# A fused attention and gated-MLP kernel: two scalar loads moved late, 24 unread TensorE products ahead of the first score product

## The chip, the core and the metric

The kernel runs on one core of one Trainium2 chip. The metric is the device time of one execution in microseconds (us); lower is better. The kernel before takes 443.92 us (median of three runs, 441.65 to 444.85).

Engines are named as in the profile: PE is TensorE (PEld its weight loads), DVE is VectorE, ACT is ScalarE, POOL is GpSimd, SP is SyncE, whose queue (SPq) issues nearly all the loads and stores here.

## What is computed

```python
# B, H, S, D = 4, 8, 768, 64; d_model 512, d_ff 1024; n_sink = 4, window = 128 (both int64 inputs)
scores = q @ k.T / sqrt(D)
keep   = (key < n_sink) | (0 <= query - key < window)
a      = softmax(where(keep, scores, -1e9))
x      = (a @ v) laid out as (B, S, H * D)
h      = relu(x @ w_in);  u, v = h[..., :512], h[..., 512:]
v_n    = (v - mean(v)) / sqrt(var(v) + 1e-6)          # over the 512 features
out    = (u * (w_spatial @ v_n + b_spatial)) @ w_out
```

The two scalars n_sink and window are run-time inputs. The kernel has a fast path for the pair (4, 128) and a general path for every other pair; the general path runs after the fast one if a flag says that the pair is another one. In the profiled run the pair is (4, 128), so only the fast path does work.

## The kernel before

Attention is cut into 48 half tiles: 4 batches, 6 tiles of 128 queries, two halves of 4 heads. For each half tile PE makes the score products (`sc`, L881 for batch 0 and L887 for the others), DVE adds the mask and takes the row maxima (`pexp` and `nm`, L892), ACT takes the exponentials (L897), the result is transposed (`tr` on PE and `pT` copies for batch 0, DMA transposes for the others), PE makes the products with v (`av`), and DVE divides (`den`, `x`, L1020 to L1024). For every tile of 128 rows there follow the product with the v half of w_in (`ps_v`, then relu, variance and the normalised `vn`), for every 256 rows the product with the u half (`ps_u`), and once a batch has all its `vn`, the spatial product (`ps_s` from `wsp` and `vn`), the gate `g`, and the last product (`ps_o`).

The weights arrive as 64-bit words. `w_in` and `w_out` are decoded in pieces of 128x512 on ACT (L663, L665), DVE (L661 or L659, L669, L671) and POOL (L674); `w_in` and `wsp` are then split into a high and a low 16-bit half on ACT (L576) and DVE (L597).

The order of all this work is made by a planner. Each piece of work is added with a rank, the engine or engines that may do it, an estimated time and the tiles that it reads and writes (`plan.add`). `Plan.order()` then goes through the pieces greedily: it takes the piece that can begin first by its own estimates, gives it the engine that would end it first, and books the ring of buffers that its tiles live in. The result is one fixed order for each engine. Each engine then works through its own instructions in order and waits where data is not there yet. PSUM has 8 banks: 4 for `sc` and `tr`, 2 for one `av` buffer, and 2 for a ring called `mm` that holds `ps_v`, `ps_u`, `ps_s`, `ps_o` and the small products of the maxima (`ps_row`, `ps_col`).

Ahead of the plan stand `begin` (masks, an identity and other constants, most of it on POOL) and `read_scalars` (L35), which loads the two scalars to all 128 partitions as 128 pieces of 8 bytes each, one load on SP's queue (L38) and one on ACT's (L39), and converts them on DVE (L41). The comparison with (4, 128) is written behind the fast path (L1211 to L1215: four comparisons, a maximum, a conversion), and every engine reads the flag into a register (L1216). On DVE the conversion and the comparison stand in the order ahead of the first `pexp`; on SP the flag is read between two loads of `w_in`. The first loads of the plan are those of the first keys (`wsp<-qk_t`, L836; for batch 0 the keys lie in room that later holds `wsp`), the first queries (`qkraw<-qk_t`, L602), and four pieces of `w_in` (`dec<-w_in`).

Of the kernel before, what the change touches and what calls it, by code (L numbers as in the profile page):

```python
# [6 lines left out]
F32 = mybir.dt.float32  # L7
F32R = mybir.dt.float32r
F16 = mybir.dt.float16
BF16 = mybir.dt.bfloat16  # L10
I32 = mybir.dt.int32
U32 = mybir.dt.uint32
AF = mybir.ActivationFunctionType
ALU = mybir.AluOpType
AX = mybir.AxisListType
# [4 lines left out]
P = 128  # L20
# [11 lines left out]
EXP_HIGH = bits_as_f32(0x47F00000)  # L32


def read_scalars(tc, pool, n_sink, window):  # L35
    nc = tc.nc
    words = pool.tile([P, 4], I32, name="words")
    nc.sync.dma_start(words[:, 0:2], n_sink.bitcast(I32).partition_broadcast(P))  # L38
    nc.scalar.dma_start(words[:, 2:4], window.bitcast(I32).partition_broadcast(P))  # L39
    wf = pool.tile([P, 4], F32, name="wf")  # L40
    nc.vector.tensor_copy(wf, words)  # L41
    return words, wf


def f64_to_f32(nc, raw, w, tmp, top=None):
# [218 lines left out]
TOGETHER0 = 4  # L264
FIRST_LOADS = (('q', 0), ('w', 0), ('w', 1), ('w', 2), ('w', 3), ('v', 0), ('q', 1), ('v', 2), ('v', 4), ('v', 5))
IN_TURN = ("u", "vn", "qkraw", "qp", "pexp", "pT", "p16", "xT", "x16", "av", "sc", "vraw", "vslot0", "vslot1", "vslot2", "vslot3")
LATENCY = {"PE": 0.25, "d": 0.15, "a": 0.18, "p": 0.12}


# [7 lines left out]


QUEUED = 3.0
class Plan:  # L280


# [4 lines left out]
    def __init__(self, rings, ring_of):  # L287
        self.pieces, self.rings, self.ring_of = [], rings, ring_of
# [5 lines left out]
    def order(self):  # L294
# [40 lines left out]
        def room(i):  # L335

            t, new = 0.0, {}
            for key in ps[i][5] + ps[i][6]:
# [4 lines left out]
                k = len(held[ring]) + new.get(ring, 0)  # L343
                if ring in IN_TURN and turn[ring][k] != base:
                    return None
# [7 lines left out]
        while open_:  # L353
            best = None
            for i in open_:
# [4 lines left out]
                if ps[i][7] and not ps[i][5]:  # L360
                    t = max(t, moved - QUEUED)
                es = ps[i][2] if ps[i][2] not in free else (ps[i][2],)
# [20 lines left out]
            if dma is None:  # L383
                end = t + d + LATENCY[e]
            else:
# [30 lines left out]
def begin(nc, pool):  # L416


    st = Begin()
    first = pool.tile([P, 1], F32, name="first")  # L420
    nc.vector.memset(first, 0.0)
    nc.scalar.activation(first, first, AF.Exp)
    st.wsp = pool.tile([P, (NT + 1) * S], F32, name="wsp")
    st.wout = pool.tile([P, 2, KC, DM], F32R, name="wout")
    st.vflat = pool.tile([P, NV * 2 * H * (D + 1)], F16, name="vring")
    st.vring = vring = st.vflat.rearrange("p (s i h d) -> p s i h d", s=NV, i=2, h=H)

    def cur_mask(m):
        nc.gpsimd.affine_select(out=m, in_=m, pattern=[[-1, P]], compare_op=ALU.is_ge,
                                fill=NEG, base=0, channel_multiplier=1)  # L430

    def prev_mask(m):
        nc.gpsimd.affine_select(out=m, in_=m, pattern=[[1, P]], compare_op=ALU.is_gt,
                                fill=NEG, base=0, channel_multiplier=-1)

    m_first = pool.tile([P, P], BF16, name="m_first")
    nc.gpsimd.memset(m_first, 0.0)
    cur_mask(m_first)
    nc.gpsimd.memset(m_first[:, :NS], 0.0)
    m_odd = pool.tile([P, 2, SEG], BF16, name="m_odd")  # L440
    m_even = pool.tile([P, 2, SEG], BF16, name="m_even")
    m_second = pool.tile([P, 2, SEG], BF16, name="m_second")
    for m, cur in ((m_odd, 1), (m_even, 0), (m_second, 1)):
        nc.gpsimd.memset(m, 0.0)
        cur_mask(m[:, cur, 2:])
        prev_mask(m[:, 1 - cur, 2:])
    nc.gpsimd.memset(m_second[:, :, :2], NEG)
    nc.gpsimd.memset(m_second[:, 0, 2:2 + NS], 0.0)

    st.ident = pool.tile([P, P], F32, name="ident")  # L450
    make_identity(nc, st.ident)
    st.ones = pool.tile([1, P], F32, name="ones")
    nc.vector.memset(st.ones, 1.0)
    mhalf = pool.tile([P, 1], F32, name="mhalf")
    nc.vector.memset(mhalf, -0.5)
    b_bc = pool.tile([P, S], F32, name="b_bc")
    st.masks = m_first, m_second, m_even, m_odd
    st.mhalf, st.b_bc = mhalf, b_bc
    return st


def fast_path(tc, st, qk, v, v0, vs, w_in, w_sp, b_sp, w_out, out):

# [1 line left out]
    nc = tc.nc  # L467
    TC = 256
    VNS = 2.0 ** 10
    with (  # L470
# [42 lines left out]
        def bank(tag):  # L513
            return lambda name: ps_all.tile([P, 512], F32, tag=tag, name=name, bufs=BANKS[tag])
# [3 lines left out]
        def next_p16(name):  # L518
# [21 lines left out]
            "sc": ("sc", bank("sc")), "tr": ("sc", bank("sc")),  # L540
            "av": ("av", lambda name: ps_all.tile([P, 1024], F32, tag="av", name=name, bufs=BANKS["av"])),
            "ps_v": ("mm", bank("mm")), "ps_u": ("mm", bank("mm")), "ps_s": ("mm", bank("mm")),
            "ps_o": ("mm", bank("mm")), "ps_row": ("mm", bank("mm")), "ps_col": ("mm", bank("mm")),
        }
        rings = {"u": UB, "vn": VNB, "vr": VB, "vraw": VRB, "vsraw": 1, "qkraw": QKB, "qp": QPB, "pexp": PEB,
                 "p16": P16B, "pT": PTB, "x": 1, "x16": 2, "xT": XTB, "g": 2, "g2": G2B,
# [2 lines left out]
        plan = Plan(rings, dict({k: r for k, (r, _) in makers.items()}, **{r: r for r in rings}))  # L549
# [277 lines left out]
        def whole(b):  # L827
            return b < WHOLE
# [330 lines left out]
                     [("ob", i)], [], dma=0.8)  # L1159


        W = WHEN
        for t in (0, 2, 4, 5):
            load_v(t)
        w_in_half(1)
# [4 lines left out]
        for i, (b, t, hf) in enumerate(subs):  # L1170
            n = TOGETHER0 if whole(b) else TOGETHER
            for h2 in range(0, HH, n):
                scores(i, b, t, hf, h2, i - W["score"] + h2 * W["pair"], n)
            weights(i, b, t, hf, i - W["split"])
            attend(i, b, t, hf, i)
            if hf == 0:
                queries_keys(b, t, early.get(("q", t), i - W["load"]) if b == 0 else i - W["load"], i - W["qk"])
                if not whole(b):
                    value(b, t, i - W["value"])
                if t == 0:  # L1180
                    v_scale(b, i - W["vscale"])
                continue
            v_half(b, t, i + W["v"])
            if t % 2:
# [17 lines left out]
def tile_kernel(tc, qk, v, v0, vs, n_sink, window, w_in, w_sp, b_sp, w_out, out):  # L1202
    nc = tc.nc
    with tc.tile_pool(name="top", bufs=1) as top:
        with tc.tile_pool(name="first", bufs=1) as pool:
            st = begin(nc, pool)
            words, wf = read_scalars(tc, top, n_sink, window)
            fast_path(tc, st, qk, v, v0, vs, w_in, w_sp, b_sp, w_out, out)
        bad = top.tile([P, 4], F32, name="bad")
        for i, x in enumerate((FAST_N, 0, FAST_W, 0)):  # L1210
            nc.vector.tensor_scalar(bad[:, i:i + 1], wf[:, i:i + 1], float(x), None, op0=ALU.not_equal)  # L1211
        flag = top.tile([P, 1], F32, name="flag")
        nc.vector.tensor_reduce(out=flag, in_=bad, axis=AX.X, op=ALU.max)
        flagi = top.tile([P, 1], I32, name="flagi")
        nc.vector.tensor_copy(flagi, flag)  # L1215
        rv = nc.values_load(flagi[0:1, 0:1], min_val=0, max_val=1)  # L1216
        with tc.If(rv > 0):
            general_path(tc, wf, qk, v, w_in, w_sp, b_sp, w_out, out)

FAST_N, FAST_W = 4, 128  # L1220

# [42 lines left out]
```

## Time and profile before

| what | us |
|---|---|
| median of three runs | 443.92 (441.65 to 444.85) |
| span of the profiled execution, first to last instruction of the program | 439.1 |
| PE busy | 414.1 (94%) |
| DVE busy | 319.1 (73%) |
| ACT busy | 272.0 (62%) |
| POOL busy | 156.6 (36%) |

The rest of a run, about 4.8 us against the median, lies around the span. The engines run beside each other, so shares of busy time do not add up; what counts is who waits for whom. The chain that ended last is 85% PE and 9% DVE by time. PE is not busy for the first 7.4 us, is partly busy up to about 40 us, and is then busy nearly all the time, with short stops between 100 and 130 us, until 432 us.

### The profile page before, as it was taken

To read this page: it belongs to the slowest core of one execution; us is meant where nothing else is said; L and a number is where in the kernel's file an instruction comes from. 1 tells how busy PE (TensorE), PEld (TensorE's weight loads), DVE (VectorE), ACT (ScalarE), POOL (GpSimd) and SP (SyncE) were. 2 spreads that over 40 slices of the span, in tenths; PEclk is the share of its full clock that TensorE was granted. 3 is DMA by queue.
4 is the path that set the end of the run, shared out by engine and by line. 5 is a ranking of instruction groups with operands and counts; after the bars stand their busy time and mean duration, and the time that the engine had idled before them with its cause. 6 is when DMAs were issued, how large, how long until landed. Compare 5 with 4: busy or idle time off the path is not lost.

```text
span 439.1 us, 9802 instructions
## 1 busy us (share of the span) xinstructions
PE 414.1 (94%) x3669; PEld 323.9 (74%) x3669; DVE 319.1 (73%) x937; ACT 272.0 (62%) x584; POOL 156.6 (36%) x214
## 2 busy tenths in 40 slices
PE   2689999999989999999999999999999999999994
PEld 1467777777677877877778878868778778688882
DVE  3999988689999885878986966788994645143430
ACT  3898978789977565469864754677664353232211
POOL 4426565645735432238351512343541112000000
PEclk9999999999999999999999999999999999999998
DMA  5999414549976784279964673567723822200011
GB/s 215 384 344 296 119 29 115 169 118 196 175 132 162 182 173 133 41 209 208 189 170 123 134 154 87 73 187 154 135 69 98 137 61 64 73 2 24 25 48 57
DMA packets 117928, 59.98 MB, mean 137 GB/s; under 512 B 100240, under 2 KB 103920, under 8 KB 117872
## 3 DMA queue, kind: packets, MB, share of 16 engines
q1 hardware_dynamic: 117728, 59.27, 55.3%
q8 instruction: 31, 0.51, 0.5%
q14 instruction: 25, 0.20, 0.1%
q10 hardware_dynamic: 144, 0.00, 0.0%
HBM read 28.58 MB, written 6.29 MB: 79 GB/s over the span
## 4 chain that ended last, share of the span: by engine, by line
PE 85%; DVE 9%; DMA 2%; issue 1%; ACT 1%; POOL 0%; SPq 0%; ACTq 0%; DVEq 0%
PE ps_s L608 21%; PE ps_o L608 16%; PE ps_v L608 13%; PE ps_u L608 12%; PE sc L887 6%; PE av L1013 4%; PE sc L881 3%; DVE pexp L892 2%; PE tr L925 2%; PE av L997 1%; PE av L999 1%; PE av L998 1%; DMA qkraw<-qk_t 1%; PE av L1005 1%; DVE wsp L597 1%
## 5 line engine op out<-in xcount | busy, mean ns | idle before, releaser
L608 PE MATMUL ps_s<-wsp,vn 128*128 128x256 f16 x864 | 101.0, 273 | 1.6 <-DVE wsp L597 0.8
L608 PEld LDWEIGHTS <-vn 128*128 128x128 f16 x864 | 82.5, 98 | 14.8 <-issue 2.7
L897 ACT ACTIVATE pexp<-pexp,nm 128x260 f32<-128x260 f32 (+1 forms) x192 | 81.2, 484 | 6.2 <-DVE nm L892 6.0
L608 PE MATMUL ps_o<-wout,g 128*128 128x512 f32 x288 | 70.2, 399 | 0.0
L608 PE MATMUL ps_u<-xT,win 128*128 128x256 f16 x576 | 69.0, 273 | 0.4 <-ACT u L1110 0.4
L608 PE MATMUL ps_v<-win,xT 128*128 128x512 f16 x288 | 66.2, 379 | 1.1 <-ACT u L1110 1.1
L608 PEld LDWEIGHTS ps_o<-wout,g 128*128 128x128 f32 x288 | 53.1, 188 | 12.8
L608 PEld LDWEIGHTS <-win 128*128 128x128 f16 x576 | 54.9, 98 | 10.0 <-issue 1.7
L1131 DVE SCALAR_TENSOR_TENSOR g<-ps_s,isc,b_bc 128x256 f32<-128x256 f32 x48 | 23.1, 481 | 39.6 <-PE ps_s L608 38.2
L608 PEld LDWEIGHTS <-xT 128*128 128x128 f16 x288 | 27.0, 98 | 31.5 <-issue 2.2
L574 ACT CAST g<-g 128x256 fp32r<-128x256 f32 x39 | 15.8, 404 | 50.5 <-DVE g L1135 48.3
L590 DVE TENSOR_TENSOR p<-pexp,p 128x1024 f16<-128x1024 f32 (+2 forms) x56 | 40.6, 747 | 8.6 <-ACT p L574 8.6
L590 POOL TENSOR_TENSOR x<-x,x 128x512 f16<-128x512 f32 x24 | 31.2, 1299 | 22.5 <-ACT x L574 21.4
L887 PE MATMUL sc<-kring,qp 64*128 64x260 f32 (+1 forms) x432 | 35.3, 296 | 0.0
L1110 ACT ACTIVATE u<-ps_u,icu 128x256 f32<-128x256 f32 x48 | 22.3, 469 | 17.2 <-PE ps_u L608 17.2
L887 PEld LDWEIGHTS sc<-kring,qp 64*128 64x128 f32 x432 | 28.1, 186 | 6.3 <-issue 4.2
L1078 POOL TENSOR_TENSOR rs<-rs,mhalf 128x1 f32<-128x1 f32 x24 | 16.2, 676 | 46.0 <-DVE rs L1072 42.5
L1157 ACT COPY ob<-ps_o 128x512 f32<-128x512 f32 x24 | 14.1, 586 | 27.9 <-PE ps_o L608 27.9
L574 ACT CAST p<-pexp 128x32 f16<-128x32 f32 (+2 forms) x52 | 30.7, 620 | 0.5
L1068 DVE BATCH_NORM_STATS2 st<-vr 128x6 f32<-128x512 f32 x24 | 16.5, 689 | 17.2 <-ACT vr L1062 17.2
L590 DVE TENSOR_TENSOR g<-g,g 128x256 fp32r<-128x256 f32 x41 | 22.5, 550 | 8.5 <-ACT g L574 7.9
L997 PE MATMUL av<-vring,pT 128*128 128x65 f16 x264 | 27.7, 193 | 0.0
(143 smaller groups left out, 762.5 us busy)
## 6 DMA issues: line engine op xcount, KB each, us to landing
qkraw<-qk_t SPq DMA_DIRECT2D x18, 512.0 KB, 4.4
out<-ob SPq DMA_DIRECT2D x24, 256.0 KB, 2.3
vraw<-v_s SPq DMA_DIRECT2D x18, 256.0 KB, 4.4
dec<-w_in SPq DMA_DIRECT2D x8, 512.0 KB, 6.9
wsp<-w_sp_t SPq DMA_DIRECT2D x6, 384.0 KB, 6.1
dec<-w_out SPq DMA_DIRECT2D x4, 512.0 KB, 4.5
wsp<-qk_t SPq DMA_DIRECT2D x6, 256.0 KB, 5.5
qkraw<-qk_t SPq DMA_DIRECT2D x6, 256.0 KB, 4.4
```

Of the source, the lines that this page charges most:

```text
L574: nc.scalar.copy(o, x)
L590: eng[e].tensor_tensor(out=o, in0=x, in1=hi, op=ALU.subtract)
L608: nc.tensor.matmul(o, a, m, start=(i == 0), stop=(i == n - 1))
L887: nc.tensor.matmul(o, qp[rows, qi, hp, :], keys(kring[:, ki], rows), start=(m == 0), stop=(m == 2))
L897: nc.scalar.activation(po, po, AF.Exp, bias=nm()[:, h2 + q:h2 + q + 1], scale=-1.0)
L997: nc.tensor.matmul(o[:, h], ph, vh, start=(t < 2 and j == 0), stop=False)
L1013: nc.tensor.matmul(o[:, h], pT[:, q * P:(q + 1) * P], v_whole(kt)[:, g:g + D + 1], start=(t < 2 and j == 0), stop=(j == nb - 1 and (t < 2 ...
L1068: nc.vector.bn_stats(s6, vr())
L1078: nc.gpsimd.tensor_tensor(out=vals["rs", i], in0=vals["rs", i], in1=mhalf, op=ALU.pow)
L1110: plan.add(r + WHEN["u relu"], "a", 0.36, lambda e: nc.scalar.activation(tl("u", (b, c0))[:, d, :], tl("ps_u", i)[:, :TC], AF.Relu, scale= ...
L1131: nc.vector.scalar_tensor_tensor(out=g(), in0=tl("ps_s", i)[:, :TC], scalar=vals["s", "sp"][1], in1=b_bc[:, t0:t0 + TC], op0=ALU.mult, op1 ...
L1157: plan.add(r + WHEN["o copy"], "a", 0.5, lambda e: nc.scalar.copy(tl("ob", i), tl("ps_o", i)), [("ps_o", i)], [("ob", i)])
```

## The change

Two things. First, the loads of the scalars, their conversion and their comparison become two pieces of the plan at rank 27 (`SCALARS_AT`): both loads on SP, the comparison on DVE. The flag is still read where its user stands, on every engine. Second, `begin` writes a tile `warm` of 128x512 bf16 numbers with an `iota` on POOL, and the plan gets one piece at rank -300, ahead of all others: 24 products of 128x128 with 128x256 of that tile into one bank of the `mm` ring. Nothing reads that bank. The rank table `WHEN` is the same.

```diff
-def read_scalars(tc, pool, n_sink, window):
-    nc = tc.nc
-    words = pool.tile([P, 4], I32, name="words")
-    nc.sync.dma_start(words[:, 0:2], n_sink.bitcast(I32).partition_broadcast(P))
-    nc.scalar.dma_start(words[:, 2:4], window.bitcast(I32).partition_broadcast(P))
-    wf = pool.tile([P, 4], F32, name="wf")
-    nc.vector.tensor_copy(wf, words)
-    return words, wf
+class Scalars:
+    def __init__(self, nc, pool, n_sink, window):
...
+    def load(self):
+        for i, x in enumerate(self.sources):
+            self.nc.sync.dma_start(self.words[:, 2 * i:2 * i + 2], x.bitcast(I32).partition_broadcast(P))
+
+    def compare(self):
+        v = self.nc.vector
+        v.tensor_copy(self.wf, self.words)
+        for i, x in enumerate((FAST_N, 0, FAST_W, 0)):
+            v.tensor_scalar(self.bad[:, i:i + 1], self.wf[:, i:i + 1], float(x), None, op0=ALU.not_equal)
+        v.tensor_reduce(out=self.flag, in_=self.bad, axis=AX.X, op=ALU.max)
+        v.tensor_copy(self.flagi, self.flag)
...
+WARM_N, WARM_FIRST = 256, 24
+SCALARS_AT = 27.0
...
+    st.warm = pool.tile([P, 512], BF16, name="warm")
+    nc.gpsimd.iota(st.warm, pattern=[[1, 512]], base=1, channel_multiplier=3, allow_small_or_imprecise_dtypes=True)
...
+        def keep_warm(n):
+            for _ in range(n):
+                nc.tensor.matmul(tl("warm", 0)[:, :WARM_N], st.warm[:, :P], st.warm[:, :WARM_N], start=True, stop=True)
+
+        plan.add(-300, "PE", 0.1, lambda e: keep_warm(WARM_FIRST), [], [("warm", 0)])
+        plan.add(SCALARS_AT, "SP", 0.8, lambda e: scalars.load(), [], [("words", 0)], dma=0.3)
+        plan.add(SCALARS_AT, "d", 1.3, lambda e: scalars.compare(), [("words", 0)], [("flag", 0)])
...
-            words, wf = read_scalars(tc, top, n_sink, window)
...
-        bad = top.tile([P, 4], F32, name="bad")
-        for i, x in enumerate((FAST_N, 0, FAST_W, 0)):
-            nc.vector.tensor_scalar(bad[:, i:i + 1], wf[:, i:i + 1], float(x), None, op0=ALU.not_equal)
...
```

The start of SP's queue, before and then with the change (`wsp<-qk_t` is the load of the first keys, `qkraw<-qk_t` that of the first queries, `dec<-w_in` a piece of 64-bit weights, `vring<-v_ones` two tiles of v):

```order
L1260 UNCONDITIONAL_BRANCH
L38 DMA words<-n_sink 128x2
L836 DMA wsp<-qk_t 128x4x128
L602 DMA qkraw<-qk_t 128x512
L602 DMA dec<-w_in 128x1024 x4
L801 DMA vring<-v_ones 128x2x520
```

```order
L1278 UNCONDITIONAL_BRANCH
L854 DMA wsp<-qk_t 128x4x128
L620 DMA qkraw<-qk_t 128x512
L620 DMA dec<-w_in 128x1024 x4
L819 DMA vring<-v_ones 128x2x520
L854 DMA wsp<-qk_t 128x4x128
```

The load of the scalar ahead of the first keys is gone; the rest stands as it did.

The last of the 24 products on PE and what follows them, with the change (before, the `sc` row is PE's first):

```order
L1182 LDWEIGHTS warm
L1182 MATMUL warm<-warm 128x256
L1182 LDWEIGHTS warm
L1182 MATMUL warm<-warm 128x256
L899 MATMUL sc<-wsp,qkraw 128x128 x8
L943 MATMUL tr<-ident,pexp 128x128 x4
L1031 MATMUL av<-vring,pT 128x65 x4
```

All 24 stand ahead of the first score products. On POOL the `iota` stands ahead of the masks.

DVE where the comparison now stands, about 63 us into the span of before (`w` is a piece of w_out being decoded, `vr` and `vn` the normalised v half), before and then with the change:

```order
L1086 TENSOR_SCALAR vr<-vr,mv,rs 128x512
L671 SCALAR_TENSOR_TENSOR w_751<-dec,w_751 128x512
L590 TENSOR_TENSOR vn<-vr,vn 128x512
L892 ISA pexp,nm<-sc,m_even 128x260
L892 ISA nm 128x1
```

```order
L1104 TENSOR_SCALAR vr<-vr,mv,rs 128x512
L689 SCALAR_TENSOR_TENSOR w_780<-dec,w_780 128x512
L52 CAST wf<-words 128x4
L54 TENSOR_SCALAR bad<-wf 128x1 x4
L55 TENSOR_REDUCE flag<-bad 128x1
L56 CAST flagi<-flag 128x1
L910 ISA pexp,nm<-sc,m_even 128x260
L910 ISA nm 128x1
```

The seven instructions of the scalars have come in, and the subtraction for `vn` has gone from here to POOL. Up to this place every engine's order is the same but for the moved and the new instructions. From here to the order's place at about 155 us in before the planner orders the pieces differently: on PE one `ps_v` and several `ps_u` groups of twelve change places with half tiles of attention, with the same number of `ps_v` and `ps_u` groups ahead of the first `ps_s`; and some pieces change engines (over the whole order DVE has two fewer 128x512 copies or casts, ACT two fewer `p16` casts of 128x1024 and two fewer `kring` casts, POOL two more casts of each of the latter two kinds). Behind that the orders are the same again.

## Rows read from the trace of the kernel before

**Rows 1.** The page, busy time of each engine: busy us, share of the span, instructions.

```profile
PE 414.1 (94%) x3669; PEld 323.9 (74%) x3669; DVE 319.1 (73%) x937; ACT 272.0 (62%) x584; POOL 156.6 (36%) x214
```

**Rows 2.** Busy time by stretch. Columns: stretch, its length; then busy us (and instructions) of PE, PEld, DVE, ACT, POOL; granted TensorE clock, share of the DMA engines, GB/s.

```profile
5.00:10.00 5.00, 2.52 (x16) 2.10 (x16) 2.44 (x17) 1.40 (x3) 0.80 (x6) 1.00 1.02 389
10.00:20.00 10.00, 5.28 (x22) 3.89 (x23) 9.72 (x30) 8.88 (x20) 5.19 (x4) 1.00 1.05 383
20.00:30.00 10.00, 8.10 (x32) 5.48 (x29) 9.50 (x35) 10.00 (x23) 1.47 (x2) 1.00 0.96 348
30.00:40.00 10.00, 9.59 (x66) 7.84 (x65) 9.38 (x32) 7.54 (x17) 5.75 (x8) 1.00 1.04 302
40.00:60.00 20.00, 20.00 (x135) 14.12 (x134) 18.71 (x61) 18.51 (x39) 12.32 (x18) 1.00 0.49 139
```

**Rows 3.** The same columns, stretches of 1 us at the start.

```profile
4.00:5.00 1.00, 0.00 (x0) 0.00 (x0) 0.00 (x0) 0.00 (x0) 0.41 (x3) 1.00 0.17 7
5.00:6.00 1.00, 0.00 (x0) 0.00 (x0) 0.36 (x5) 0.00 (x0) 0.00 (x0) 1.00 0.96 293
```

**Rows 4.** The timeline of the start: start us, us, engine, line, operation, out<-in, count, and in brackets the idle time before it and what ended it.

```profile
0.72 0.20 POOL L437 MEMSET m_first<- 128x128 bf16 x1 [0.29 <-POOLq L1254]
0.72 0.40 SPq L38 DMA_DIRECT2D words<-n_sink  x1
1.90 0.60 SPq L602 DMA_DIRECT2D qkraw<-qk_t  x1
2.20 0.31 POOL L444 MEMSET m_second<- 128x260 bf16 x1
4.12 0.29 POOL masks.py:199 TENSOR_SCALAR_AFFINE_SELECT ident<-ident 128x128 f32<-128x128 f32 x1
5.60 0.17 DVE L41 CAST wf<-words 128x4 f32<-128x4 int32 x1 [4.59 <-DMA words<-n_sink]
6.36 0.15 DVE L1215 CAST flagi<-flag 128x1 int32<-128x1 f32 x1
7.43 2.70 PE L881 MATMUL sc<-wsp,qkraw 64*128 64x128 f32 x16 [7.43 <-DMA qkraw<-qk_t]
8.35 0.29 DVE L892 CUSTOM_DVE_ANT_0 pexp<-sc,m_first 128x128 f32<-128x128 f32 x1 [1.83 <-PE sc L881]
```

**Rows 5.** DMA issues of the stretch 0 to 2.5 us, and (last row) of 49 to 51 us: out<-in, queue, operation, count, KB, us from issue to landing.

```profile
qkraw<-qk_t SPq DMA_DIRECT2D x1, 256.0 KB, 5.4
words<-n_sink SPq DMA_DIRECT2D x1, 1.0 KB, 4.8
...
qkraw<-qk_t SPq DMA_DIRECT2D x1, 256.0 KB, 3.5
```

**Rows 6.** PE's timeline, the same form of product early and later (columns as in rows 4).

```profile
29.46 1.91 PE L925 MATMUL tr<-ident,pexp 128*128 128x128 f32 x8
...
39.83 1.04 PE L925 MATMUL tr<-ident,pexp 128*128 128x128 f32 x8
```

**Rows 7.** The chain that ended last, stretch 0 to 45 us, in order of time: start us, us, what; and its rows at 60.76 us and at 85.16 us, where the first score products of batch 1 begin.

```profile
21.06 3.98 DMA wsp<-qk_t
...
25.08 2.68 PE sc L881 x7
...
60.76 2.62 PE ps_u L608 x24
...
85.16 0.81 PE sc L887 x12
```

**Rows 8.** The page, POOL's costliest 128x512 operation: busy us, mean ns, idle before it.

```profile
L590 POOL TENSOR_TENSOR x<-x,x 128x512 f16<-128x512 f32 x24 | 31.2, 1299 | 22.5 <-ACT x L574 21.4
```

**Rows 9.** SP and DVE at 44 and around 64 us (timeline), and SP's read of the flag (one line's instructions: count, ns least/median/most, first and last start us).

```profile
43.68 1.26 SPq L1041 DMA_TRANSPOSE xT<-x  x1
...
64.52 0.39 SPq L602 DMA_DIRECT2D qkraw<-qk_t  x1
...
63.12 1.55 DVE L590 TENSOR_TENSOR vn<-vr,vn 128x512 f16<-128x512 f32 x1 [0.35 <-ACT vn L574]
64.59 0.41 DVE L892 CUSTOM_DVE_ANT_0 pexp<-sc,m_even 128x260 f32<-128x260 f32 x1
...
L1216 SPq TENSOR_LOAD <-flagi x1: 476/476/476, 15.2 to 15.2; - x1
```

**Rows 10.** What PE waited for from 42 to 160 us (us, times, longest), and two rows of POOL and the chain there.

```profile
PE ps_v L608 <- ACT u L1110: 1.1, 1, 1.1
PE ps_s L608 <- DVE wsp L597: 0.8, 1, 0.8
PE ps_s L608 <- ACT wsp L576: 0.5, 1, 0.5
PE ps_u L608 <- ACT u L1110: 0.4, 1, 0.4
PE ps_s L608 <- DVE g L1131: 0.3, 1, 0.3
PE ps_col L635 <- DVE allmax L632: 0.3, 1, 0.3
...
128.18 2.12 PE ps_s L608 x18
...
110.70 2.06 POOL L590 TENSOR_TENSOR p<-pexp,p 128x1024 f16<-128x1024 f32 x1
```

More of the change, by code (lines that the diff above doesn't have):

```diff
@@ L32 @@
 EXP_HIGH = bits_as_f32(0x47F00000)
-def read_scalars(tc, pool, n_sink, window):
-    nc = tc.nc
-    words = pool.tile([P, 4], I32, name="words")
-    nc.sync.dma_start(words[:, 0:2], n_sink.bitcast(I32).partition_broadcast(P))
-    nc.scalar.dma_start(words[:, 2:4], window.bitcast(I32).partition_broadcast(P))
-    wf = pool.tile([P, 4], F32, name="wf")
-    nc.vector.tensor_copy(wf, words)
-    return words, wf
+class Scalars:
+    def __init__(self, nc, pool, n_sink, window):
+        self.nc, self.sources = nc, (n_sink, window)
+        self.words = pool.tile([P, 4], I32, name="words")
+        self.wf = pool.tile([P, 4], F32, name="wf")
+        self.bad = pool.tile([P, 4], F32, name="bad")
+        self.flag = pool.tile([P, 1], F32, name="flag")
+        self.flagi = pool.tile([P, 1], I32, name="flagi")
+    def load(self):
[8 more added lines that the diff above has]
+        v.tensor_copy(self.flagi, self.flag)
 def f64_to_f32(nc, raw, w, tmp, top=None):
@@ L459, in begin, with fast_path @@
     return st
-def fast_path(tc, st, qk, v, v0, vs, w_in, w_sp, b_sp, w_out, out):
+def fast_path(tc, st, scalars, qk, v, v0, vs, w_in, w_sp, b_sp, w_out, out):
     nc = tc.nc
@@ L542, in fast_path @@
             "ps_v": ("mm", bank("mm")), "ps_u": ("mm", bank("mm")), "ps_s": ("mm", bank("mm")),
-            "ps_o": ("mm", bank("mm")), "ps_row": ("mm", bank("mm")), "ps_col": ("mm", bank("mm")),
+            "ps_o": ("mm", bank("mm")), "warm": ("mm", bank("mm")), "ps_row": ("mm", bank("mm")), "ps_col": ("mm", bank("mm")),
         }
@@ L1206, in tile_kernel @@
             st = begin(nc, pool)
-            words, wf = read_scalars(tc, top, n_sink, window)
-            fast_path(tc, st, qk, v, v0, vs, w_in, w_sp, b_sp, w_out, out)
-        bad = top.tile([P, 4], F32, name="bad")
-        for i, x in enumerate((FAST_N, 0, FAST_W, 0)):
-            nc.vector.tensor_scalar(bad[:, i:i + 1], wf[:, i:i + 1], float(x), None, op0=ALU.not_equal)
[L1212 to L1216, printed above, removed]
+            scalars = Scalars(nc, top, n_sink, window)
+            fast_path(tc, st, scalars, qk, v, v0, vs, w_in, w_sp, b_sp, w_out, out)
+        rv = nc.values_load(scalars.flagi[0:1, 0:1], min_val=0, max_val=1)
         with tc.If(rv > 0):
-            general_path(tc, wf, qk, v, w_in, w_sp, b_sp, w_out, out)
+            general_path(tc, scalars.wf, qk, v, w_in, w_sp, b_sp, w_out, out)
 FAST_N, FAST_W = 4, 128
```

## The prediction, made before the changed kernel was run

> **What bounds the kernel now.** I read the page first for the shares: PE is busy 94% of the span, and the other engines far less [rows 1]. A share over the whole span hides that the start is another regime, so I went on to the busy time by stretch. The reader is to see three regimes there. Up to about 5 us nothing of weight runs. From 10 to 40 us DVE is the fullest engine, with 9.72, 9.50 and 9.38 us busy of 10, while PE has 5.28, 8.10 and 9.59. From 40 us on PE is busy in all of 20 us [rows 2]. Work gained or lost ahead of 40 us therefore moves the end of the kernel as a whole, since PE behind it has no idle time to take it up; and what counts ahead of 40 us is when DVE's stream begins and how often it stops.
>
> Then I looked at what lets that stream begin. In the timeline of the start DVE's first `pexp` begins at 8.35 us, 0.92 us behind PE's first product at 7.43 us, and PE was released by the load of the first queries [rows 4]. That load was issued at 1.90 us and landed 5.4 us later; a lone load of the same 256 KB at about 50 us took 3.5 us [rows 5]. Between 4 and 5 us the DMA engines moved 7 GB/s, and from 5 to 6 us 293 [rows 3]. The load of one scalar, 1 KB in pieces of 8 bytes, stands ahead of it on the same queue and takes 4.8 us to land [rows 5]. So the queue seems to give its first microseconds to the small pieces.
>
> **Part 1: the scalars leave the start.** SP issues the load of the first queries one issue earlier. The scalar's issue takes 0.40 us and the next begins at most 0.1 us behind it, so I take 0.46 us, and the load is issued at 1.44 us. If it still takes 5.4 us it lands at 6.8 us; if it takes the 3.5 us of the lone load, at 4.9 us. These are the two ends; before it was 7.3 us (1.90 + 5.4). The second scalar's load leaves ACT's queue, where it took an issue and delayed nothing that the first products need. On DVE the conversion and comparison ran from 5.60 to 6.51 us (6.36 + 0.15) [rows 4], when DVE had nothing else to do, so taking them from there gains nothing by itself.
>
> **Part 2: 24 products ahead of the first.** They wait for the `iota` of 128x512 on POOL. The trace has none. From below, a memset of 128x260 takes 0.31 us [rows 4], so 0.6 us for 512; from above, POOL's two-input operation on 128x512 takes 1.30 us [rows 8]. Begun at 0.72 us, where POOL's masks begin now [rows 4], it ends between 1.3 and 2.0 us. I take 1.6, since an iota reads nothing and writes like the memset but has to count. For a product the nearest row is `ps_u`: 24 of them, also with 256 columns of 16 bits, take 2.62 us at 60.76 us [rows 7]. But early products are slower: eight `tr` products of one form take 1.91 us at 29.46 us and 1.04 us at 39.83 us, a factor of 1.84 [rows 6]. The granted clock reads 1.00 in every stretch of the start [rows 2], which does not agree with these durations; I go by the durations and take the start to run at the low level, 1.2 GHz, until some time between 30 and 40 us, and at 2.4 GHz behind. So the 24 take 2.6 us at the high level and 4.8 us at the low one (2.62 x 1.84). With the iota they end at 1.6 + 4.8 = 6.4 us, with ends of 3.9 us (1.3 + 2.6) and 6.8 us (2.0 + 4.8).
>
> The first score product then begins when both the load and the 24 are through. I take 6.4 us, which is the end of the 24 at the low level and also lies within the load's two ends. That is 1.0 us earlier than 7.43. The ends are 4.9 us (2.5 earlier) and 6.8 us (0.6 earlier). The masks that the first `pexp` needs move back on POOL by the iota; POOL's preparation ended at 4.41 us (4.12 + 0.29) [rows 4], so with 1.3 us more it ends at 5.7 us, still ahead of a `pexp` at 7.3 us. If the load were at 4.9 us and the 24 at 3.9 us this cover would be gone.
>
> **Part 3: DVE's stops.** From 10 to 40 us DVE is idle for 0.28 + 0.50 + 0.62 = 1.40 us [rows 2]. Some of it hangs on loads: PE begins at 25.08 us with keys that were issued at 21.06 us and took 3.98 us [rows 7], against 3.5 us for a lone load. The loads now start up to 2.4 us earlier while DVE starts 1.0 us earlier, so loads have a longer lead than before. I take half of the idle time as given back, 0.7 us, with ends of nothing and 1.4 us.
>
> **Part 4: the scalars at their late place.** On SP two issues of 0.40 us stand behind the transpose at 43.68 us [rows 9], with SP free behind them. Landing in at most 4.8 us [rows 5], the words are there long before DVE comes to them at about 63 us. On DVE the seven instructions cost the 0.91 us that they took at the start. In their place `vn<-vr,vn` of 1.55 us at 63.12 us goes to POOL [rows 9], so the four `pexp` queued behind the comparison do not come later than 64.59 us. On SP the flag's read, 0.48 us, waits for the comparison, and a load of queries that was issued at 64.52 us stands behind it [rows 9]. It slips by under 1 us, and its queries are first multiplied at 85.16 us [rows 7]. I cost part 4 at nothing.
>
> **Part 5: another order from about 65 to 155 us.** PE's work ahead of the first `ps_s` (128.18 us, [rows 10]) is the same. PE's named waits from 42 to 160 us come to 3.4 us [rows 10], nearly all where DVE and ACT prepare `wsp` and the gate. DVE and ACT lose some casts to POOL, which helps there, while POOL's operations of this size are long (2.06 us for 128x1024 [rows 10]). The most to gain is these 3.4 us. For a loss the nearest rows are one such POOL operation and one `kring` operation of about 1.3 us (by rows 8) in series, 3.4 us as well. I take zero between two equal ends.
>
> **The sum.** 1.0 + 0.7 = 1.7 us off the span of 439.1 us gives 437.4 us. The profiled execution's span is 4.8 us under the median of the runs shown, 443.92 us; what lies around the span does not change, so I predict 443.92 - 1.7 = **442.2 us**.
>
> **A rule weighed against the rows.** The rows show low-level durations until about 30 us and PE busy for only 5.28 us from 10 to 20 us, with the first products behind it. The Trainium skill, page "TensorE: Matmul & The Clock Gate", section "What's actually happening", says that the array starts at half its clock and that activity releases it. The same page's section "HAM oscillation — how this bites in real kernels" says that idle gaps between bursts bring the low clock back. By the first rule alone the 24 products lift the start to the high level and rival 1 below comes true; by the second they lift it for the first products only, which is the forecast. PE's half-empty stretch from 10 to 20 us is on the side of the second, and no run here has yet shown the first.
>
> **Rivals.**
>
> 1. *The clock rises during the 24 and stays up, and the load lands early.* For it: the 24 are PE's first dense stretch, 128 rows deep. Against it: PE has little to do from 10 to 20 us. The first product is then at 4.9 us (2.5 earlier), the first `pexp` follows 0.5 us behind it rather than 0.92 (0.92 / 1.84; 0.4 more), and all of DVE's 1.40 us of stops goes: 4.3 us, so 439.6 us.
> 2. *The gain is taken up, or the change doesn't do what it says.* The 24 end no earlier than the load did (iota and low level together at 6.8 us, plus DVE's own backlog), or the bulk loads start at 5 us whatever stands ahead of them, and the crossover from 95 to 128 us, where PE waits 3.4 us for DVE and ACT, waits that much longer. Then 443.9 us, give or take 0.7.
> 3. *Slower: the new order delays the first `ps_s`.* PE cannot begin it before the last `wsp` split and the last `vn`. If one more `p` operation (2.06 us) and one `kring` operation (1.3 us) on POOL come to stand in that chain, it is 3.4 us later, and 443.9 - 1.7 + 3.4 = 445.6 us. It decides from a delay of 1.7 us on. For it: POOL gets longer work there. Against it: DVE and ACT, which end those waits now, get less.
>
> **How the numbers follow.** Forecast 0.45 (its own range 441.1 to 443.3: 0.6 to 1.4 us at the start, 0 to 1.4 us of DVE's stops), rival 1 0.2, rival 2 0.2, rival 3 0.15. The range reaches from a little under rival 1, with a part of the 3.4 us back as well, to rival 3: 438.8 to 445.6. One per cent, 4.4 us, is about what a measurement can tell from no change. Under 439.5 us lies about half of rival 1: 0.12. Over 448.3 us it takes rival 3 twice over: 0.03. The rest, 0.85, is within 1%.
>
> **What would show it.** Step 1: bulk DMA ahead of 5 us in the first windows, and the first queries landing at 4.9 to 6.8 us. Step 2: the 24 ending near 6.4 us at about 0.2 us each, and the first `sc` right behind. Step 3: under 1.4 us of DVE idle time from 10 to 40 us. Step 5: PE's waits from 42 to 160 us at 3.4 us, and the first `ps_s` 1.7 us earlier than 128.18. The prediction is wrong if `tr` products at 12 to 30 us run at the late duration (rival 1), if the shift at 40 us is gone at 130 us (rivals 2 and 3), or if the `iota` takes 3 us or more.

## The result and the profile after

The changed kernel takes 446.6 us (median of 20 runs, 443.18 to 451.27), the kernel before 442.44 us (median of 20 runs, 440.15 to 445.54). The ratio is 1.0078 [1.0056, 1.0101]: 0.8% slower. The forecast was 442.2 us with a range of 438.8 to 445.6, so direction and range are both missed.

The ratio leaves out the five slow runs above 450 us (with them it is 1.011, by the means of all twenty), and the profiled execution (450.67 us, span 448.9 us) is one of the five, so its rows are read for where time goes and the ratio for how much. Lines of the changed kernel stand 18 further down than in before where the code is the same.

The page, busy time of each engine, answers to [rows 1]:

```profile
PE 425.0 (95%) x3693; PEld 332.1 (74%) x3693; DVE 322.3 (72%) x934; ACT 270.0 (60%) x583; POOL 161.8 (36%) x219
```

PE has 24 products more, and is busy 10.9 us longer than before: more than those 24 take (4.47 us below), so other products take longer.

The timeline of the start answers to [rows 4], the DMA issues of 0 to 2.6 us to [rows 5], the busy time by 1 us to [rows 3]:

```profile
0.82 0.56 POOL L440 IOTA warm<- 128x512 bf16 x1 [0.40 <-POOLq L1272]
1.44 4.47 PE L1182 MATMUL warm<-warm 128*128 128x256 bf16 x24 [1.44 <-POOL warm L440]
5.84 0.72 PE L899 MATMUL sc<-wsp,qkraw 64*128 64x128 f32 x8
6.49 0.29 DVE L910 CUSTOM_DVE_ANT_0 pexp<-sc,m_first 128x128 f32<-128x128 f32 x1 [5.47 <-PE sc L899]
9.21 0.66 ACT L681 ACTIVATE w<-dec 128x512 f32<-128x512 f32 x1 [6.99 <-DMA dec<-w_in]
9.90 0.69 DVE L679 TENSOR_SCALAR_CACHE_REDUCE w<-w 128x512 f32<-128x512 f32 x1 [2.48 <-ACT w L681]
```

```profile
dec<-w_in SPq DMA_DIRECT2D x2, 512.0 KB, 7.8
wsp<-qk_t SPq DMA_DIRECT2D x1, 256.0 KB, 3.3
qkraw<-qk_t SPq DMA_DIRECT2D x1, 256.0 KB, 3.2
```

```profile
3.00:4.00 1.00, 1.00 (x7) 0.69 (x6) 0.00 (x0) 0.00 (x0) 1.00 (x7) 1.00 1.26 403
4.00:5.00 1.00, 1.00 (x7) 0.74 (x6) 0.00 (x0) 0.00 (x0) 1.00 (x7) 1.00 0.47 113
5.00:6.00 1.00, 1.00 (x11) 0.73 (x10) 0.00 (x0) 0.00 (x0) 0.70 (x7) 1.00 0.57 217
8.00:9.00 1.00, 0.00 (x0) 0.00 (x0) 0.00 (x0) 0.00 (x0) 0.00 (x0) 1.00 0.92 225
```

The first half of the change does what its parts say. The queries land 3.2 us after their issue instead of 5.4, the bulk moves from 3 us on, and DVE's first `pexp` starts 1.86 us earlier (6.49 against 8.35). The queries are there at 4.7 us (issued at 1.47 us), so it is the 24 products, which end at 5.91 us, that set the first score product. Then DVE stops for 2.48 us: ACT's first piece of `w_in` begins at 9.21 us. The DMA engines started two microseconds earlier and then moved less: 269 GB/s over 5 to 10 us, where [rows 2] have 389. Over the whole of the first 10 us the mean is 198 GB/s, against 196 before: by then the same 2.0 MB have been moved.

Busy time by stretch (columns as in [rows 2]), and PE's `tr` products, which answer to [rows 6]:

```profile
5.00:10.00 5.00, 2.68 (x25) 2.02 (x22) 1.03 (x9) 0.79 (x2) 0.70 (x7) 1.00 0.90 269
10.00:20.00 10.00, 4.54 (x17) 3.46 (x19) 9.71 (x29) 8.95 (x21) 5.03 (x4) 0.59 0.99 353
20.00:30.00 10.00, 7.92 (x31) 5.21 (x30) 9.54 (x38) 10.00 (x23) 1.56 (x3) 0.50 0.92 297
30.00:40.00 10.00, 10.00 (x46) 8.48 (x46) 8.34 (x26) 5.54 (x13) 3.78 (x4) 0.50 1.09 348
97.00:101.00 4.00, 4.00 (x26) 2.97 (x27) 3.89 (x6) 1.39 (x4) 2.46 (x2) 0.57 0.64 189
131.00:138.00 7.00, 5.27 (x42) 4.01 (x42) 5.75 (x20) 5.06 (x12) 2.62 (x3) 0.51 0.27 71
```

```profile
37.43 1.91 PE L943 MATMUL tr<-ident,pexp 128*128 128x128 f32 x8
43.67 1.04 PE L943 MATMUL tr<-ident,pexp 128*128 128x128 f32 x8
```

Here the granted clock is recorded from the first products on, and the low level shows: 0.59, 0.50, 0.50. In this execution it lasts past 40 us, and PE is full at the low level from 30 to 40 us (before, `tr` was fast at 39.83 us already). Two more low stretches stand in the middle of the kernel, around 97 to 101 and 131 to 138 us.

What PE waited for from 42 to 165 us (us in total, times, longest), against [rows 10]:

```profile
PE ps_s L626 <- DVE wsp L615: 2.5, 1, 2.5
PE ps_s L626 <- ACT vr L1080: 1.9, 1, 1.9
PE ps_u L626 <- ACT vr L1080: 0.7, 1, 0.7
PE ps_v L626 <- DVE allmax_r L657: 0.4, 1, 0.4
PE ps_v L626 <- DMA xT<-x: 0.2, 1, 0.2
```

5.7 us instead of 3.4, and 4.4 of it in one place, around the first `ps_s`. A comparison of the starts of the `ps` groups on PE's timelines gives the account (first `ps_v` of before, then first `ps_v` and third `ps_s` group of the changed kernel):

```profile
41.22 2.76 PE L608 MATMUL ps_v<-win,xT 128*128 128x512 f16 x12
45.07 2.76 PE L626 MATMUL ps_v<-win,xT 128*128 128x512 f16 x12
138.06 2.13 PE L626 MATMUL ps_s<-wsp,vn 128*128 128x256 f16 x18
```

The first `ps_v` is 3.8 us later than before (41.2 to 45.1), this difference stands until about 75 us, and from the third `ps_s` group on (128.18 us in [rows 10], 138.06 now) it is 9.9 us and stays near that to the end. So in this execution some 3.8 us are lost ahead of 41 us and 6.1 us between 75 and 138 us. (The prediction called the row at 128.18 the first `ps_s`; the first group of before begins at 121.33.)

### The profile page after: what moved, and what is told of

It is laid out like the page before. It is cut to its first block, busy times and chain, and to the rows that moved or that the text cites. A ratio compares the mean times of both kernels' runs of the same rounds, so it can differ in the third digit from the quotient of the medians.

```text
span 448.9 us, 9855 instructions
## 1 busy us (share of the span) xinstructions
PE 425.0 (95%) x3693; PEld 332.1 (74%) x3693; DVE 322.3 (72%) x934; ACT 270.0 (60%) x583; POOL 161.8 (36%) x219
## 4 chain that ended last, share of the span: by engine, by line
PE 86%; DMA 5%; DVE 5%; ACT 2%; issue 1%; SPq 1%; ACTq 0%
PE ps_s L626 21%; PE ps_o L626 15%; PE ps_v L626 13%; PE ps_u L626 11%; PE sc L905 6%; PE av L1031 5%; PE sc L899 3%; PE tr L943 2%; DMA dec<-w_in 2%; PE av L1015 2%; PE av L1017 2%; PE av L1016 2%; DMA qkraw<-qk_t 1%; PE av L1023 1%; DVE pexp L910 1%; DMA wsp<-qk_t 1%
## 5 line engine op out<-in xcount | busy, mean ns | idle before, releaser
L626 PE MATMUL ps_s<-wsp,vn 128*128 128x256 f16 x864 | 102.8, 276 | 4.7 <-DVE wsp L615 2.5
L626 PEld LDWEIGHTS <-vn 128*128 128x128 f16 x864 | 83.4, 99 | 18.6 <-issue 5.6
L626 PE MATMUL ps_u<-xT,win 128*128 128x256 f16 x576 | 70.1, 275 | 0.7 <-ACT vr L1080 0.7
L626 PEld LDWEIGHTS <-win 128*128 128x128 f16 x576 | 55.2, 99 | 10.9 <-issue 2.2
L608 DVE TENSOR_TENSOR p<-pexp,p 128x1024 f16<-128x1024 f32 (+2 forms) x56 | 41.7, 770 | 7.1 <-ACT p L592 7.1
L608 DVE TENSOR_TENSOR g<-g,g 128x256 fp32r<-128x256 f32 x41 | 23.9, 584 | 8.5 <-ACT g L592 7.9
L592 ACT CAST p<-pexp 128x32 f16<-128x32 f32 (+2 forms) x50 | 28.8, 603 | 1.1 <-DMA pT<-p 0.6
```

What stands on the lines that cost most here:

```text
L592: nc.scalar.copy(o, x)
L608: eng[e].tensor_tensor(out=o, in0=x, in1=hi, op=ALU.subtract)
L626: nc.tensor.matmul(o, a, m, start=(i == 0), stop=(i == n - 1))
```

## The experiments

The stretch of 75 to 138 us is where the planner's new order lies. My theory after the result: the new order costs, and the products and late loads do not; the rival: they cost, through the start. The first four kernels separate the order from the instructions.

**Order alone.** Before, with three pieces in the plan that issue nothing, so that the planner makes the order of the changed kernel:

```diff
         W = WHEN
+        plan.add(-300, "PE", 0.1, lambda e: None, [], [("warm", 0)])
+        plan.add(27.0, "SP", 0.8, lambda e: None, [], [("words", 0)], dma=0.3)
+        plan.add(27.0, "d", 1.3, lambda e: None, [("words", 0)], [("flag", 0)])
```

> The kernel before, with three empty pieces in the plan where the change has its own (the 24 products, the scalar loads, the comparison): the new order from about 65 us on, but scalars loaded at the start and no extra product. Order theory (the new order makes the crossover to batch 1 longer): 2 to 5 us slower than before, PE's waits from 42 to 160 us over 5 us, the shift appearing between 75 and 140 us. Clock theory (the 24 products disturb TensorE's clock and the order costs nothing): within 1 us of before. Load theory (the earlier bulk loads bring the w_in pieces later): within 1 us of before, first w_in piece at 8.6 us as before.

449.83 us, ratio 1.0153 [1.0109, 1.0196]. An order with no instruction added or moved out of the start costs at least as much as the whole change. The size is less sure than the sign: of the six runs two took 445.28 and 445.98 us and four 449.62 to 450.26 us, and only the one at 445.98 us was profiled. Its span is 444.2 us, 5.1 us (1.2%) over that of before's profile; what the other four lose beyond that isn't shown. Its windows and PE's timeline at `ps_s` (in this execution the start is as in before; the third `ps_s` group is 6.0 us late):

```profile
93.00:97.00 4.00, 4.00 (x27) 3.00 (x26) 3.73 (x6) 1.46 (x4) 2.46 (x2) 0.57 0.70 196
127.00:134.00 7.00, 5.12 (x39) 3.94 (x39) 5.74 (x19) 4.91 (x12) 2.62 (x3) 0.53 0.25 64
```

```profile
126.61 0.38 PE L608 MATMUL ps_s<-wsp,vn 128*128 128x256 f16 x2 [2.80 <-DVE wsp L597]
128.88 4.00 PE L608 MATMUL ps_s<-wsp,vn 128*128 128x256 f16 x18 [1.90 <-ACT vr L1062]
```

The 18 products behind the stops take 4.00 us; [rows 10] have 18 in 2.12.

**Late scalars, no products.** The changed kernel without the `iota` and the 24 products (new order):

```diff
-        plan.add(-300, "PE", 0.1, lambda e: keep_warm(WARM_FIRST), [], [("warm", 0)])
+        plan.add(-300, "PE", 0.1, lambda e: None, [], [("warm", 0)])
```

> The changed kernel without the 24 products and without the iota; scalars late, new order. Order theory: as slow as the changed kernel, 3 to 4 us over before. Clock theory: back to before or 1 to 2 us faster. Load theory: if the 24 products slow the loads down, the first decode on ACT begins at about 6.5 us; if the early start of the bulk itself does it, at about 9.2 us as in the changed kernel.

449.28 us, ratio 1.0151 [1.0109, 1.0194], with the same two waits (2.8 and 1.9 us). That is more than the 3 to 4 us expected; 2.8 us of it in the profiled execution (449.22 us) are lost ahead of the first `ps_v` (44.02 us against 41.22), where the order is still that of before. ACT's first decode begins at 7.10 us, between the two times that the load theory gave.

**Products alone.** Before, in its own order and with its early scalars, and the `iota` and the 24 products ahead of the plan:

```diff
         with tc.manual_schedule():
+            for _ in range(24):
+                nc.tensor.matmul(tl("warm", 0)[:, :256], st.warm[:, :P], st.warm[:, :256], start=True, stop=True)
```

> The kernel before with the iota and the 24 products ahead of PE's first product, in the order of before, scalars loaded at the start. Order theory: within 1 us of before. Clock theory: 2 to 5 us slower than before, the granted clock rising at about 5 us, falling at about 12 us, and rising again behind 32 us in some of the runs. Load theory: within 1 us of before, since the bulk loads start at 5 us as before.

441.42 us, ratio 0.999 [0.9969, 1.001].

**Both in the old order.** All instructions of the changed kernel, in the order of before, with load and comparison put in by hand and the three pieces gone from the plan:

```diff
+            keep_warm(WARM_FIRST)
-            for f, e in order:
+            for k, (f, e) in enumerate(order):
+                if k == LOAD_AT:
+                    scalars.load()
+                if k == COMPARE_AT:
+                    scalars.compare()
                 f(e)
```

> Scalars late and the 24 products, but every engine in the order of before: loads and comparison put in by hand at the places where the plan has them in the changed kernel, ahead of everything that changed places. Order theory: within 1 us of before, or up to 1 us faster by the earlier first product. Clock theory: as slow as the changed kernel, 3 to 4 us. Load theory: 0.6 us slower, the first decode on ACT at 9.2 us.

441.38 us, ratio 0.9984 [0.9955, 1.0013]. The rival falls: in the order of before the change's instructions cost nothing that can be told, so the loss comes from the order.

What in the order costs? The rows at the first `ps_s`, of before and of the changed kernel (timelines of DVE, POOL and ACT):

```profile
120.63 0.74 DVE L597 SCALAR_TENSOR_TENSOR vring<-vraw,v_scale,vring 128x512 f16<-128x512 f32 x1
120.77 0.68 ACT L1062 ACTIVATE vr<-ps_v,icv 128x512 f32<-128x512 f32 x1
116.11 1.90 POOL L590 TENSOR_TENSOR kring<-qkraw,kring 128x512 fp32r<-128x512 f32 x1
124.20 1.48 POOL L590 TENSOR_TENSOR x<-x,x 128x512 f16<-128x512 f32 x1 [6.19 <-ACT x L574]
```

```profile
126.93 2.55 DVE L615 SCALAR_TENSOR_TENSOR vring<-vraw,v_scale,vring 128x512 f16<-128x512 f32 x1
129.40 1.00 DVE L615 SCALAR_TENSOR_TENSOR wsp<-wsp,wsp_scale 128x768 f16<-128x768 f32 x1
126.50 2.43 POOL L608 TENSOR_TENSOR p<-pexp,p 128x1024 f16<-128x1024 f32 x1 [2.19 <-ACT p L592]
131.48 0.62 ACT L592 CAST x<-x 128x512 f16<-128x512 f32 x1 [3.48 <-DVE x L1042]
132.00 0.68 ACT L1080 ACTIVATE vr<-ps_v,icv 128x512 f32<-128x512 f32 x1
```

In before POOL is idle from 118.0 to 124.2 us, DVE's split `vring` takes 0.74 us there, and `vr`, which frees the bank that the second `ps_s` group needs, runs at 120.77 us, before that group is due. In the new order a subtraction for `p` runs on POOL beside the same split, the split ends 0.55 us after POOL's operation and takes 2.55 us, and the last `wsp` split waits behind it. On ACT `vr` stands behind the cast of `x`, which waits for DVE. Four edits of order_alone test these two and the clock.

**The relu early.** The comments in this cut and the next are added here.

```diff
         order = plan.order()
+        order.insert(642, order.pop(648))   # icv, DVE
+        order.insert(643, order.pop(653))   # vr<-ps_v, ACT: now ahead of the cast of x
```

> The kernel of order_alone (new order, scalars early, no products), with one relu (vr from ps_v, the one that releases the bank of the second ps_s group) moved ahead of the x cast on ACT, and the tiny icv product it needs moved ahead on DVE. In order_alone PE waits 2.8 us for the last wsp split, then 1.9 us for this relu, and the granted clock is at the low level from about 127 to 134 us. Theory A (the waits cost, and the clock falls because PE stopped for so long): the 1.9 us wait goes; if the low stretch stays it is 1.9 us faster than order_alone, ratio to before about 1.011; if the low stretch goes too, 3.4 us more, ratio about 1.003. Rival (these waits are only where PE shows a delay that DVE's chain sets anyway): another wait of about 1.9 us takes its place and the ratio stays at 1.015.

444.78 us, ratio 1.0075 [1.0042, 1.0107]. The wait for `vr` is gone and, in the profiled execution, the low stretch too (window 127 to 134 us):

```profile
122.35 2.72 POOL L590 TENSOR_TENSOR p<-pexp,p 128x1024 f16<-128x1024 f32 x1 [1.89 <-ACT p L574]
123.08 2.01 DVE L788 TENSOR_TENSOR icv<-v_inv,win_inv 128x1 f32<-128x1 f32 x1
126.73 2.34 PE L608 MATMUL ps_s<-wsp,vn 128*128 128x256 f16 x20 [2.87 <-DVE wsp L597]
127.00:134.00 7.00, 7.00 (x87) 6.12 (x85) 6.86 (x20) 5.52 (x13) 3.70 (x5) 1.00 0.26 71
```

The second row came unasked: `icv`, one number a partition, 0.15 us in order_alone, now stands first on DVE beside POOL's subtraction and takes 2.01 us, while the split behind it is back at 0.74.

**The subtraction on DVE.**

```diff
         order = plan.order()
+        order.insert(660, (order.pop(649)[0], "d"))   # p<-pexp,p: DVE, behind the statistics
```

> The kernel of order_alone with one subtraction for p (128x1024) moved from POOL to DVE, behind the statistics of the first gate. In order_alone this operation runs on POOL from 122.65 to 125.08 us, and a DVE split of v beside it takes 2.54 us instead of the 0.74 us of the kernel before, with the last wsp split queued behind it. Theory A (POOL's operation holds DVE's up): the DVE split takes 0.74 us, PE's wait for wsp falls from 2.8 to about 1.0 us, the wait for vr stays near 1.9 us; 1.8 us faster than order_alone, ratio about 1.011, or about 1.004 if the granted clock does not fall then. Rival (that split is long for another reason): it still takes about 2.5 us, and the ratio stays at 1.015 or gets worse, since DVE has 1.2 us more to do.

444.5 us, ratio 1.005 [1.0027, 1.0074].

```profile
125.88 0.74 DVE L597 SCALAR_TENSOR_TENSOR vring<-vraw,v_scale,vring 128x512 f16<-128x512 f32 x1
127.60 0.38 PE L608 MATMUL ps_s<-wsp,vn 128*128 128x256 f16 x2 [1.01 <-DVE wsp L597]
129.88 1.44 PE L608 MATMUL ps_s<-wsp,vn 128*128 128x256 f16 x6 [1.90 <-ACT vr L1062]
```

The split is at 0.74 us, the wait for `wsp` at 1.01, the wait for `vr` unchanged, all as theory A has it. The clock still falls in the profiled execution, but less (0.76 over 127 to 134 us, against 0.53).

**Both edits.** The two diffs above together.

> The kernel of order_alone with both edits of relu_early and add_on_dve. Theory A: PE's waits around the first ps_s fall from 4.7 us to about 1.0 us, 3.7 us faster than order_alone with the low clock stretch left (ratio about 1.007), 7.1 us faster if the low stretch of 6.8 us goes as well (ratio about 0.999). Rival: the new order loses elsewhere, so that the ratio stays above 1.010.

443.18 us, ratio 1.0032 [1.0, 1.0063]. Both waits are down to 1.1 us in all; a wait of 1.6 us of a `ps_v` for a gate on DVE is new, and a low stretch stands between 85 and 93 us (clock 0.79 there).

**Zero products in the stops.** A weight tile of zeros, added into the sum that waits:

```diff
+                if i == (0, 0, 0):
+                    z = (st.zero, wsp[:, 0, 0, t0:t0 + TC])
+                    pairs = pairs[:16] + [z] * 22 + pairs[16:17] + [z] * 16 + pairs[17:]
                 three(tl("ps_s", i)[:, :TC], pairs)
```

> The kernel of order_alone with 38 products of a zero weight tile put into the first ps_s group, 22 ahead of the product that waits for the last wsp split and 16 ahead of the last one, so that PE works through its two stops (2.8 and 1.9 us) without changing the sum. At 0.11 us each they take 2.4 and 1.75 us, about as long as the stops. They move no work of DVE or ACT. Theory A (the clock falls because PE stops): the granted clock stays at 1.00 from 127 to 134 us, and the 6.8 us of low level give back 3.4 us: ratio about 1.008. Rival (the low stretch comes whatever PE does there, or its cost is hidden): the low stretch stays, the ratio stays at 1.015 or above.

444.03 us, ratio 1.0041 [1.0015, 1.0068].

```profile
123.72 2.56 PE L610 MATMUL ps_s<-wsp,zero 128*128 128x256 f16 x22
126.80 1.91 PE L610 MATMUL ps_s<-wsp,zero 128*128 128x256 f16 x16
128.97 2.12 PE L610 MATMUL ps_s<-wsp,vn 128*128 128x256 f16 x18 [0.15 <-ACT vr L1064]
127.00:134.00 7.00, 6.85 (x80) 5.89 (x80) 6.88 (x21) 5.73 (x13) 2.62 (x3) 1.00 0.27 69
```

PE's second `ps_s` group starts when it did in order_alone (128.97 against 128.88), so nothing of the waiting is shorter; but it takes 2.12 us instead of 4.00. Products that add nothing to the sum made the kernel faster, by the clock: 5.12 us busy at a clock of 0.53 are 2.4 us, and the spans of the two profiles differ by 2.1 us (444.2 and 442.1), 0.5%. The medians differ by more (449.83 and 444.03), but order_alone ran on another chip than these four, and four of its six runs lie some 4 us above the profiled one. So the four edits are better compared by the spans of profiles that start like before: order_alone is 1.2% over before's span, relu_early 0.8%, relu_and_add 0.4% and zero_fill 0.7%.

**One number in the plan.** In the plan alone, without a run, one can see which of the three pieces moves the order: with the comparison's estimated time at 0.9 us or less the planner keeps the order of before, with 1.3 us it makes the new one, at every rank tried from 20 to 80.

```diff
-        plan.add(SCALARS_AT, "d", 1.3, lambda e: scalars.compare(), [("words", 0)], [("flag", 0)])
+        plan.add(SCALARS_AT, "d", 0.9, lambda e: scalars.compare(), [("words", 0)], [("flag", 0)])
```

> The changed kernel with one number different: the comparison's estimated time in the plan is 0.9 us, which is what its seven instructions take on DVE in the trace, instead of 1.3 us. The planner then gives the order of before around it, so the first ps_s should come without the waits of 2.8 and 1.9 us and without the low clock stretch behind them. Theory A (the order is the cause): ratio to before 0.998, as both_old_order had it. Rival (the products or the late scalars cost): 1.008, as the changed kernel has it.

442.3 us, ratio 1.0013 [0.9994, 1.0032]: the loss of 1.0078 is gone. On each engine this kernel has the same order as both_old_order, so 0.9984 and 1.0013 are two measurements of one thing: no change that can be told.

**Late scalars in the old order.** both_old_order without `keep_warm` and the `iota`:

```diff
-            keep_warm(WARM_FIRST)
```

> The scalars late, no products, and the order of before. In late_no_products ACT's first piece of w_in began at 7.10 us, 1.5 us earlier than in before, and DVE's first at 7.80 us; with the products they began at 9.21 and 9.90 us. Theory A (the products do nothing for the time outside the new order): ratio 0.997 to 1.000. Rival (the late scalars by themselves cost something that the products cover, as late_no_products at 1.015 against the changed kernel at 1.008 suggests): 1.004 to 1.008.

441.49 us, ratio 0.9997 [0.9966, 1.0028]. The late scalars cost nothing that can be told. DVE's first `pexp` starts at 5.51 us here, 2.84 us earlier than before and 0.98 us earlier than with the 24 products, and then DVE stops for 2.41 us for the first piece of `w_in`:

```profile
8.17 0.66 ACT L679 ACTIVATE w<-dec 128x512 f32<-128x512 f32 x1 [5.95 <-DMA dec<-w_in]
5.00:10.00 5.00, 2.25 (x16) 1.66 (x14) 2.04 (x11) 1.79 (x4) 0.19 (x2) 1.00 0.94 270
```

**New order with products, early scalars.** Before, with the three pieces of order_alone, of which the first now issues the 24 products (and with their `iota`):

```diff
+        plan.add(-300, "PE", 0.1, lambda e: [nc.tensor.matmul(tl("warm", 0)[:, :256], st.warm[:, :P], st.warm[:, :256], start=True, stop=True) for _ in range(24)], [], [("warm", 0)])
```

> The new order with the 24 products, the scalars early as in before. order_alone had 1.015, late_no_products (scalars late, new order) 1.015, the changed kernel (scalars late, products, new order) 1.008. Theory P (the products themselves give back about 0.7 per cent in the new order): about 1.008. Theory S (they do so only with the scalars late): about 1.015. In either case PE's waits of about 2.8 and 1.9 us at the first ps_s stay; what differs would be how long the granted clock is at the low level ahead of 150 us.

445.28 us, ratio 1.0107 [1.0064, 1.0149]. It lies between the two theories, and its interval touches both: whether the products themselves give something back in the new order stays open.

## Why the prediction failed

**Part 5 is the step that failed:** "I take zero between two equal ends", of 3.4 us each. The order alone cost 1.5% in order_alone's six runs, and 1.2% by the spans of the profiles; there the start is as in before, and 6.0 us are lost between 75 and 134 us. Three things stand in place of the zero. First, two waits of PE, 2.8 and 1.9 us. Second, the larger one comes from an operation given to POOL: I counted this as help for DVE ("DVE and ACT lose some casts to POOL, which helps there"), while on the chip DVE's split waited until POOL's was done. Third, behind the stops the granted clock falls, and PE is busy for 5.12 us at 0.53. That term was missing altogether, so my end of 3.4 us was too small. By busy time times missing clock the two low stretches of order_alone cost 2.4 us (5.12 x 0.47) and 1.7 us (4.00 x 0.43), and PE's named waits are 2.4 us above before's (5.8 against 3.4): 6.5 us, against the 6.0 measured. Rival 3 had the place and the sign (445.6 us, chance 0.15), and it had a `p` operation of POOL in the chain. But it put it in series with work that needs it; in fact the splits don't use its result, and DVE waited for it all the same.

The Trainium skill, page "SBUF — State Buffer", section "SBUF: two separate sides", says that DVE and GpSimd share a pair of ports as an exclusive lock: a DVE operation with two SBUF inputs and a GpSimd operation that reads SBUF don't run side by side, and the later one blocks until the first is done. The trace agrees: 0.74 us became 2.55, and 0.15 became 2.01, each ending just after POOL's operation. The planner of this kernel keeps such a port too, but in its own time: it had put POOL's subtraction behind the splits, and on the chip POOL, which waits for data and not for the plan's time, came first.

**Part 1 was right in its mechanism and took the gain at the queue too small:** the queries took 3.2 us to land, less than the lone load's 3.5. **Part 2** was right: the `iota` took 0.56 us (forecast about 0.9), the 24 took 4.47 us (forecast 4.8, low level), the first `pexp` came 1.86 us earlier instead of 1.0. The 24 hold that up by about 1 us: without them it comes at 5.51 us (late_old_order).

**Part 3 failed in its sign:** instead of giving back half of the 1.40 us, the earlier start met a longer wait for `w_in`. With the scalars late the DMA engines moved 269 to 294 GB/s from 5 to 10 us in five profiles, against 389 in [rows 2], and the first piece of `w_in` began on ACT at 7.10 to 9.21 us, around the 8.60 of before. I took the loads to start earlier and run as fast; they started earlier and ran slower. DVE's idle time from 10 to 40 us, which I had at 0.7 us, is 2.4 us in the changed kernel and 1.6 to 2.1 in the three profiles in the old order with late scalars. In these three, 0.4 to 0.9 us are left of the 1.0 + 0.7 at the first `ps_v`. At the end of the kernel the full 1.7 us would be a ratio of 0.996, which the interval of cost_0_9 excludes and that of both_old_order does not. Why the rate is lower was not tried.

**Part 4 was right:** the seven instructions took 0.91 us on DVE (66.52 to 67.43), SP's read of the flag 0.47 us, and in cost_0_9 a lead of 0.8 us at the first `ps_v` is still 0.8 us at 117 us, with the comparison in between.

**The clock:** rival 1 is excluded. The high level of the first products is gone again in the window of 10 to 20 us (0.59), as the forecast had it. But the time at which it comes back differs between executions: the first `ps_v` is 2.8 us late in the profiles of late_no_products and add_on_dve too, which have no products, and on time or early in the other experiments. In these two, eight `tr` products still take 1.91 us at 36.4 and 36.7 us, where in before they take 1.38 us at 34.83 us already. So the 3.8 us of the profiled execution at 41 us (0.6 by `w_in`, the rest put down to the clock) need no products to come about; whether the products or the new order make them more frequent isn't shown. One part is not settled: a low stretch near 85 to 101 us, which is the second of the two counted above (1.7 us), stands in six of the eight profiles of the new order and in none of the five of the old one, though PE shows no stop there.

**The 4.8 us around the span** were a wrong reading: the profiled run of the changed kernel took 450.67 us at a span of 448.9, so 1.8 us lie around it. By these 1.8 us the profiled execution of before, with its span of 439.1 us, took about 440.9 us and was one of the faster ones. The base of the forecast, 443.92 us from three runs, is also 1.5 us above the 442.44 us of twenty. The difference between the kernels is not touched by either.

No version here beats before by more than can be told; cost_0_9 undoes the whole loss with one number.

## What to carry to other kernels

A piece added to a greedy planner is priced by the order that it makes, not by its instructions: 0.4 us in an estimate made the difference between a ratio of 1.0013 and one of 1.0078. Give the planner measured times (0.91 us here, not 1.3), and when the order moves in a tight place, read there which POOL operation now runs beside a two-input DVE operation and what stands ahead of the operation that frees a PSUM bank. Where a stop of PE can't be removed, products of zeros in the same sum are worth a try: here they kept the granted clock at 1.00.

## What the hardware showed that I had not expected

- A 128x1 operation on DVE took 2.01 us instead of 0.15 because POOL was at work beside it; the profile shows it as busy time of DVE, not as a wait.
- Two stops of PE of 2.8 and 1.9 us brought the granted clock to 0.53 over the 7 us from 127 us on, in a kernel that had been at 1.00 since 97 us; 38 products of zeros in them kept it at 1.00. With one stop of 2.87 us alone (relu_early) it stayed at 1.00 as well.
- Bulk loads that began 2 us earlier moved 269 to 294 GB/s from 5 to 10 us instead of 389: over the first 10 us the mean is 198 to 225 GB/s in the five profiles, against 196 before.
